# Three raw weight buffers, one buffer of converted words, and the bounds of w of eight units checked later, in an RWKV kernel with two feed-forward layers

## The chip, the cores and the metric

The kernel runs on 1 core of one Trainium2 chip. The metric is the device time of one execution in microseconds. A core has TensorE (PE; its weight loads are listed as PEld), VectorE (DVE), ScalarE (ACT), GpSimd (POOL) and SyncE (SP), which here issues all the DMAs. Each engine works through its own queue in order; an instruction that waits holds up everything behind it on that engine.

## The reference

Inputs are r, k, v, w of shape 4 x 8 x 768 x 48 (batch, heads, sequence, head size), u of 8 x 48, and the weights of two feed-forward layers. The attention keeps a 48 x 48 state for each batch and head:

```python
for t in range(S):
    cur = u * k[t] outer v[t]
    y[t] = r[t] @ (state + cur)
    state = w[t][:, None] * state + k[t] outer v[t]
```

The result, as 3072 tokens by 384, goes through two layers:

```python
h = x @ w_in                     # 384 -> 2048
x = (h - np.tanh(h)) @ w_out     # 2048 -> 384
h = x @ w_in2                    # 384 -> 1024
e = exp(h - max(h)); sm = e / (sum(e) + 1e-9)
solu = h * sm
out = (layernorm(solu) * g_ln) @ w_out2
```

The weights reach the kernel as 64-bit floats.

## The kernel before, in words

**Units and blocks.** The attention is cut into 24 units of 128 tokens and 8 heads (`UB` = 4 units make a block of 512 tokens, `NB` = 6 blocks). A unit u goes through `att_pre` (ruk on GpSimd, its sum dg on VectorE), `att_0` (transposes, the running product inc, its logarithm and exponential kh), `att_1`, `att_2` (the products qk and the transposed keys kt, copied by ScalarE to kn at L319), `att_3` (the state update ds at L328, L329, then L339, L340 on VectorE) and `att_4` (the output y at L354, copied to xs by ScalarE at L359 and VectorE at L360). Units 0 to 3 run in the prologue, from the sorted list `first`. The rest run between the steps of the first layer.

**Steps.** The loop over s has one step for each block i and each of the `NM` = 16 chunks m of 128 hidden columns. `part1` (L395) makes hp with nine matmuls of 128 x 512 (L401): each factor is held as a high and a low part, three products for each of three row groups. Then the nonlinearity is made as a polynomial: t on ScalarE (L406), y on VectorE (L407), a second square on ScalarE (L410), y on VectorE (L412), and a check of the range on ScalarE (L413), whose result is only its accumulated flag. g is split into high and low parts (L415 or L417, and L418 on GpSimd). In the first and the last block L410 writes over hp, in the others a tile with the tag q. `part2` (L421) adds chunk m to x2p two steps later, with nine matmuls (L425). Step s = 0 of unit work and step 0 of the layer are offset so that a unit runs in every four steps.

**Weights.** The 64-bit weights are loaded as words into a raw tile of 128 x 1536 words (`load_pair`, L149; four DMAs of 96 KB at L367 and one of 384 KB at L384) and converted (`convert`, L112). ScalarE rescales the low words in place (L121). VectorE masks and shifts the high words into a PSUM bank (L129, L130) and adds both into a tile of converted words, cv_x (L131), in two halves. ScalarE copies cv_x to the high part of wa (L134) and GpSimd subtracts that from cv_x for the low part (L135). There are two raw tiles (pool `cvr`) and two cv_x tiles (pool `cv`). Conversion m is that of chunk m. Conversions 0 and 1 are in the prologue, conversion s + 2 in step s of the first block (L657, L658), so that `part1` of block 0 follows the conversions closely. From step 16 on the raw tiles take the weights once more for a check of their range (`check_pair`, L143), 24 of them. In the last block the second layer's eight pairs are loaded and converted (`conv_b`, L459) through the same pools; there cv_x serves for the intermediate words too.

**Checks of w.** Bounds of w are checked unit by unit (`check_w`, L239) with two Relu on ScalarE, one for each bound, each with an accumulated flag. For units 0 to 7 (`TURN` = 8) they stand in `att_pre`, on the loaded w, with a scratch tile (cw, ruk or inv) as output; in units 4 to 7 that scratch tile is the one into which GpSimd then writes ruk (L254). From unit 8 on they read the turned w in PSUM (L282). At the end of the first layer the flags are added up, and if one is set, a general path runs in place of the result.

**What sets the order.** The program is traced in the order of the lists and loops; a scheduler then orders each engine's queue by when it estimates that operands and buffers are ready, and adds the waits. `issue_after` puts instructions behind a named one on the same engine. A tile of a pool is reused when all readers of its last content are done. All DMAs are in SyncE's queue, in order.

The last part, from about 560 us, is the second layer for 24 tiles of 128 tokens; its tiles lie where the pools of the first layer were.

Of the kernel before, what the change touches and what calls it, by code (L numbers as in the profile page):

```python
# [33 lines left out]
TURN = 2 * UB  # L34


W_LO, W_HI = 0.75, 1.34
# [21 lines left out]
class Kern:  # L59
# [7 lines left out]
    def setup(self, const):  # L67
        nc = self.nc
        self.ident = const.tile([128, 128], F32, name="ident")
        self.zeros = const.tile([128, 1], F32, name="zeros")  # L70
        self.ub = const.tile([128, H, D], F32, name="ub")
        self.mask = const.tile([128, 4, 128], U8, name="mask")
        self.cst = const.tile([128, 8], F32, name="cst")
        self.nflag = 2 * NU + NB * NM + NM + NM2
        self.flags = const.tile([128, self.nflag], F32, name="flags")
        make_identity(nc, self.ident)
        nc.vector.memset(self.zeros, 0.0)
        for i, val in enumerate((F_SB, -F_T2, W_LO, -W_HI, -0.5, P_SB, P_MIN, FLAG_MIN2)):
            nc.vector.memset(self.cst[:, i:i + 1], val)
        (self.c_fsb, self.c_t2, self.c_lo, self.c_hi, self.c_mhalf, self.c_sb, self.c_min,  # L80
         self.c_flag) = (self.cst[:, i:i + 1] for i in range(8))

    def setup_mask(self, ones):
        nc = self.nc
        nc.gpsimd.memset(ones, 1.0)
        nc.gpsimd.affine_select(
            out=ones, in_=ones, compare_op=ALU.is_gt, fill=0.0, base=0,
            pattern=[[0, 4], [1, 128]], channel_multiplier=-1,
        )
        nc.vector.tensor_copy(self.mask, ones)  # L90
# [21 lines left out]
    def convert(self, pool, raw, hi, lo, scale=None, bank=None):  # L112
# [10 lines left out]
        for i in range(n):  # L123
# [7 lines left out]
            v.tensor_tensor(x[:, s], a, L_[:, s], ALU.add)  # L131
# [11 lines left out]
    def check_pair(self, rpool, n):  # L143

        raw = self.load_pair(rpool, n)
        with self.tc.issue_after(self.last_act.ins):
            self.check(raw, 2 * NU + NB * NM + n)
# [13 lines left out]
    def att_setup(self, att, xp0, xp1):  # L161
# [27 lines left out]
        for t in self.vt:  # L189
            nc.gpsimd.memset(t[:, :, D:64], 0.0)  # L190

# [47 lines left out]
    def check_w(self, u, w, tmp):  # L239
        for i, (b, s) in enumerate(((self.c_lo, -1.0), (self.c_hi, 1.0))):  # L240
            self.nc.scalar.activation(tmp, w, AF.Relu, bias=b, scale=s,
                                      accum_out=self.flags[:, 2 * u + i:2 * u + i + 1])

    def att_pre(self, u):
# [6 lines left out]
        if u < TURN:  # L251
            w = self.gp.tile([128, BLK], F32, tag="q", name="cw")[:, 0:DM].rearrange("p (h d) -> p h d", h=H) if u < UB else ruk
            self.check_w(u, t[:, 2, :, 0:D], w)
# [47 lines left out]
    def att_2(self, u):  # L301
# [11 lines left out]
        for e in range(2):  # L313
            v.copy_predicated(self.aq[:, e], self.mask, ps[e])
# [27 lines left out]
    def att_4(self, u):  # L342
# [16 lines left out]
        nc.scalar.copy(xs[:, 0, :, cols], p[:, 0:KM])  # L359
        v.tensor_tensor(xs[:, 1, :, cols], p[:, 0:KM], xs[:, 0, :, cols], ALU.subtract)  # L360
# [34 lines left out]
    def part1(self, i, m):  # L395
# [7 lines left out]
        q = self.gp.tile([128, BLK], F32, tag="q", name="q")  # L403
# [7 lines left out]
        col = 2 * NU + i * NM + m  # L411
# [9 lines left out]
    def part2(self, i, m, gs):  # L421
# [5 lines left out]
        if m == NM - 1:  # L427
            for d in range(KM):
                o = self.gp.tile([128, BLK], F32, tag="qty"[d], name="x2o")
                self.nc.scalar.activation(o, self.x2p[d], AF.Copy, scale=-1.0)  # L430
                self.nc.sync.dma_start(out=self.x2d[d * 128:(d + 1) * 128, i * BLK:(i + 1) * BLK], in_=o)
# [161 lines left out]
def fast_path(tc, K, const):  # L593
# [9 lines left out]
    cv = pool(L, "cv", 2)  # L603
    cvr = pool(L, "cvr", 2)
# [34 lines left out]
    for s in range(-2, NB * NM + 2):  # L639
# [17 lines left out]
        if 0 <= s < NM - early:  # L657
            K.conv_a(cv, cvr, s + early)  # L658
# [19 lines left out]
        if 0 <= n < NM + NM2 and due < 3:  # L678
# [220 lines left out]
```

## Time and profile before

| | us |
|---|---|
| median of 3 runs | 770.36 (769.48 to 771.55) |
| the profiled execution | 775.22 |
| its span, first to last instruction | 773.4 |
| PE busy | 725.0 (94%) |
| DVE busy | 585.2 (76%) |
| ACT busy | 490.8 (63%) |
| POOL busy | 419.0 (54%) |

Times in the trace count from the start of the span. Busy shares are means over stages that differ: the prologue and the first block (to about 160 us), the other blocks (to about 560 us) and the second layer. PEclk is the granted clock of TensorE as a share of its full 2.4 GHz. The end of a matmul in the trace is modelled, so rows of many matmuls overlap a little.

### The profile page before, as it was taken

To read this page: it belongs to the slowest core of one execution; us is meant where nothing else is said; L and a number is where in the kernel's file an instruction comes from. 1 tells how busy PE (TensorE), PEld (TensorE's weight loads), DVE (VectorE), ACT (ScalarE), POOL (GpSimd) and SP (SyncE) were. 2 spreads that over 40 slices of the span, in tenths; PEclk is the share of its full clock that TensorE was granted. 3 is DMA by queue.
4 is the path that set the end of the run, shared out by engine and by line. 5 is a ranking of instruction groups with operands and counts; after the bars stand their busy time and mean duration, and the time that the engine had idled before them with its cause. 6 is when DMAs were issued, how large, how long until landed. Compare 5 with 4: busy or idle time off the path is not lost.

```text
span 773.4 us, 13992 instructions
## 1 busy us (share of the span) xinstructions
PE 725.0 (94%) x4882; PEld 599.2 (77%) x4882; DVE 585.2 (76%) x999; ACT 490.8 (63%) x920; POOL 419.0 (54%) x397
## 2 busy tenths in 40 slices
PE   6558988999999999999999999999989999999986
PEld 4446667778877888887888887878769989989976
DVE  4868888877766687677677774487669999999992
ACT  4436777588676877686768665787745555554552
POOL 7424575666566666556655654467525454454440
PEclk9879999999999999999999999999999999999999
DMA  9962666666756756576555510232045555555631
GB/s 156 189 127 69 157 185 151 147 169 179 175 146 162 196 143 174 133 205 177 138 154 168 155 62 11 82 123 83 10 158 183 168 178 172 175 169 168 188 104 46
DMA packets 171632, 110.80 MB, mean 143 GB/s; under 512 B 93600, under 2 KB 160288, under 8 KB 171552
## 3 DMA queue, kind: packets, MB, share of 16 engines
q1 hardware_dynamic: 171552, 109.82, 52.9%
q8 instruction: 40, 0.66, 0.4%
q14 instruction: 40, 0.33, 0.1%
HBM read 88.81 MB, written 20.97 MB: 142 GB/s over the span
## 4 chain that ended last, share of the span: by engine, by line
PE 49%; DVE 28%; ACT 10%; DMA 5%; SPq 4%; issue 3%; POOL 1%; ACTq 0%; DVEq 0%; POOLq 0%
PE hp L401 19%; PE x2p L425 19%; DVE tw L539 6%; DVE so L514 4%; PE y L354 4%; DVE e L508 4%; DMA raw<-in_moe_w_out_dram 3%; ACT e L515 3%; DVE part L504 3%; PE qk L312 3%; SPq L367 2%; PE o L564 2%; DVE cv_x L131 2%; SPq L201 1%; PE kt L318 1%
## 5 line engine op out<-in xcount | busy, mean ns | idle before, releaser
L425 PE MATMUL x2p<-g,wa 128*128 128x512 f32 x864 | 226.0, 400 | 9.6 <-ACT g L415 7.9
L401 PE MATMUL hp<-xs,wa 128*128 128x512 f32 x864 | 216.0, 395 | 2.5 <-POOL wa L135 1.3
L425 PEld LDWEIGHTS x2p<-g,wa 128*128 128x128 f32 x864 | 158.7, 189 | 49.6 <-ACT g L415 9.9
L401 PEld LDWEIGHTS hp<-xs,wa 128*128 128x128 f32 x864 | 163.4, 190 | 39.7 <-POOL wa L135 2.3
L418 POOL TENSOR_TENSOR g<-y,g 128x512 fp32r<-128x512 f32 x96 | 129.6, 1351 | 48.4 <-ACT g L415 39.0
L407 DVE TENSOR_TENSOR y<-hp,t 128x512 f32<-128x512 f32 x96 | 65.8, 686 | 76.8 <-ACT t L406 60.4
L564 PE MATMUL o<-wb,ts 128*128 128x384 f32 x576 | 105.1, 336 | 2.5 <-POOL ts L543 2.5
L482 PE MATMUL h<-wb,x2s 128*128 128x512 f32 x432 | 104.1, 392 | 3.2 <-POOL x2s L471 1.7
L413 ACT ACTIVATE q<-t,cst 128x512 f32<-128x512 f32 x96 | 69.5, 724 | 55.7 <-DVE y L412 55.1
L564 PEld LDWEIGHTS o<-wb,ts 128*128 128x128 f32 x576 | 100.7, 188 | 4.8 <-POOL ts L543 3.2
L482 PEld LDWEIGHTS h<-wb,x2s 128*128 128x128 f32 x432 | 80.4, 188 | 20.7 <-POOL x2s L471 2.7
L417 POOL TENSOR_SCALAR g<-y 128x512 fp32r<-128x512 f32 x64 | 40.3, 630 | 81.5 <-DVE y L412 77.4
L406 ACT ACTIVATE t<-hp 128x512 f32<-128x512 f32 x96 | 56.5, 588 | 27.2 <-PE hp L401 26.3
L515 ACT ACTIVATE e<-so 128x1024 f32<-128x1024 f32 x24 | 25.5, 1061 | 59.6 <-DVE so L514 59.6
L543 POOL TENSOR_TENSOR ts<-tw,ts 128x512 fp32r<-128x512 f32 x44 | 55.9, 1292 | 4.4 <-ACT ts L542 4.4
L412 DVE SCALAR_TENSOR_TENSOR y<-q,y 128x512 f32<-128x512 f32 x64 | 51.4, 803 | 2.9
L471 POOL TENSOR_TENSOR x2s<-x2s 128x384 fp32r<-128x384 f32 x24 | 24.4, 1017 | 48.1 <-ACT x2s L470 43.7
L297 POOL TENSOR_TENSOR inv<-inc,kh 112x512 f32<-112x512 f32 x24 | 29.1, 1213 | 37.4 <-ACT kh L289 33.7
L410 ACT ACTIVATE q<-t,cst 128x512 f32<-128x512 f32 x64 | 46.3, 723 | 1.3
L539 DVE STREAM_TRANSPOSE tw<-sw 128x1024 f32<-128x1024 f32 x22 | 44.5, 2022 | 0.4 <-issue 0.3
L517 POOL TENSOR_TENSOR st<-st,cst 128x1 f32<-128x1 f32 x23 | 12.6, 549 | 53.0 <-DVE st L498 45.3
L121 ACT ACTIVATE raw<-raw 128x768 uint32<-128x768 uint32 x24 | 21.8, 908 | 27.9 <-DMA raw<-in_moe_w_out_dram 24.3
(138 smaller groups left out, 1182.4 us busy)
## 6 DMA issues: line engine op xcount, KB each, us to landing
raw<-in_moe_w_out_dram SPq DMA_DIRECT2D x48, 384.0 KB, 4.0
raw<-in_moe_w_in_dram SPq DMA_DIRECT2D x128, 96.0 KB, 2.8
dso<-so SPq DMA_DIRECT2D x22, 512.0 KB, 3.0
sw<-dso SPq DMA_DIRECT2D x88, 128.0 KB, 3.0
rkw<-in_k_dram SPq DMA_DIRECT2D x64, 96.0 KB, 2.7
rkw<-in_r_dram SPq DMA_DIRECT2D x64, 96.0 KB, 2.4
rkw<-in_w_dram SPq DMA_DIRECT2D x64, 96.0 KB, 2.4
raw<-in_moe_w_in_dram SPq DMA_DIRECT2D x16, 384.0 KB, 3.2
```

Of the source, the lines that this page charges most:

```text
L401: self.mm(hp, self.wa[:, a, m, j * 128:(j + 1) * 128], xs[:, b, j], start=n == 0, stop=n == len(seq) - 1)
L406: nc.scalar.activation(t, hp, AF.Square)
L407: v.tensor_tensor(y, hp, t, ALU.mult)
L412: self.last_dve = v.scalar_tensor_tensor(y, p, F_E, y, ALU.add, ALU.mult)
L413: self.last_act = nc.scalar.activation(q, t, AF.Relu, bias=self.c_t2, accum_out=self.flags[:, col:col + 1])
L418: g.tensor_tensor(gs[:, 1], y, gs[:, 0], ALU.subtract)
L425: self.mm(self.x2p[d], self.wa[:, a, m, sl], gs[:, b], start=m == 0 and n == 0, stop=m == NM - 1 and n == 2)
L482: self.mm(p[:, f], xs[:, a, j], w, start=q == 0, stop=q == 8)
L515: nc.scalar.activation(e, so, AF.Square, accum_out=va)
L539: self.turned = nc.vector.transpose(x.rearrange("p k (t b) -> p b k t", b=4), sw)
L543: nc.gpsimd.tensor_tensor(ts[:, 1, k], x[:, k], ts[:, 0, k], ALU.subtract)
L564: self.mm(p, ts[:, a, k], self.wb[:, b, k, DM:], start=q == 0, stop=q == 3 * NM2 - 1)
```

## The change

- The pool of raw tiles has three buffers and that of converted words one.
- Where the bank is not given (second layer), L131 writes the sum into the high words of the raw tile, so that cv_x is free after it; L133, L134 and L135 then read every second word of the raw tile.
- The bounds of w become one: the square of w - 1.045 must not be over 0.087025. It is one Square and one Relu with a flag, in place of two Relu.
- Units 0 to 7 are no longer checked in `att_pre`. Two more `check_pair` (after the 24 for weights) load the w of four units each into a raw tile, with four DMAs, and check 128 x 1536 words with one Square and one Relu.
- Conversion 2 (step s = 0) is traced under `behind()`: its ScalarE instructions stand behind L359 of unit 3 and its VectorE instructions behind L360 of unit 3.
- The tag q has one buffer in place of two.
- The mask is one 128 x 128 tile, broadcast over four in `att_2`; the zeros share a tile with the flags, of which there are fewer.

```diff
--- before.py
+++ after.py
@@ -32,9 +32,10 @@
 RKW = 3 * H * 64
 ROW = 4 * 4 * D
 TURN = 2 * UB
-
-
-W_LO, W_HI = 0.75, 1.34
+NW = NU - TURN + TURN // UB
+
+
+W_MID, W_RAD2 = 1.045, 0.087025
 
 P_MIN = 1e-30
 
@@ -67,17 +68,17 @@
     def setup(self, const):
         nc = self.nc
         self.ident = const.tile([128, 128], F32, name="ident")
-        self.zeros = const.tile([128, 1], F32, name="zeros")
         self.ub = const.tile([128, H, D], F32, name="ub")
-        self.mask = const.tile([128, 4, 128], U8, name="mask")
+        self.mask = const.tile([128, 128], U8, name="mask")
         self.cst = const.tile([128, 8], F32, name="cst")
-        self.nflag = 2 * NU + NB * NM + NM + NM2
-        self.flags = const.tile([128, self.nflag], F32, name="flags")
+        self.nflag = NW + NB * NM + NM + NM2
+        flags = const.tile([128, self.nflag + 1], F32, name="flags")
+        self.flags, self.zeros = flags[:, 0:self.nflag], flags[:, self.nflag:]
         make_identity(nc, self.ident)
         nc.vector.memset(self.zeros, 0.0)
-        for i, val in enumerate((F_SB, -F_T2, W_LO, -W_HI, -0.5, P_SB, P_MIN, FLAG_MIN2)):
+        for i, val in enumerate((F_SB, -F_T2, -W_MID, -W_RAD2, -0.5, P_SB, P_MIN, FLAG_MIN2)):
             nc.vector.memset(self.cst[:, i:i + 1], val)
-        (self.c_fsb, self.c_t2, self.c_lo, self.c_hi, self.c_mhalf, self.c_sb, self.c_min,
+        (self.c_fsb, self.c_t2, self.c_mid, self.c_rad, self.c_mhalf, self.c_sb, self.c_min,
          self.c_flag) = (self.cst[:, i:i + 1] for i in range(8))
 
     def setup_mask(self, ones):
@@ -87,7 +88,7 @@
             out=ones, in_=ones, compare_op=ALU.is_gt, fill=0.0, base=0,
             pattern=[[0, 4], [1, 128]], channel_multiplier=-1,
         )
-        nc.vector.tensor_copy(self.mask, ones)
+        nc.vector.tensor_copy(self.mask, ones[:, 0])
 
     def to_f32(self, pool, raw, out, scale=None, add=None):
 
@@ -128,7 +129,9 @@
                 a = bank.tile([128, 4, C], F32, tag="a", name="cv_a").rearrange("p j t -> p (j t)")[:, 0:DM].bitcast(U32)
             v.tensor_scalar(a, H_[:, s], 3, 0x3FFFFFF8, ALU.logical_shift_left, ALU.bitwise_and)
             v.scalar_tensor_tensor(a, H_[:, s], 0xC0000000, a, ALU.bitwise_and, ALU.bitwise_or)
-            v.tensor_tensor(x[:, s], a, L_[:, s], ALU.add)
+            v.tensor_tensor(H_ if bank is None else x[:, s], a, L_[:, s], ALU.add)
+        if bank is None:
+            xf = H_.bitcast(F32)
         if scale is not None:
             nc.scalar.activation(xf[:, DM:], xf[:, DM:], AF.Copy, scale=scale)
         nc.scalar.copy(hi, xf)
@@ -142,9 +145,20 @@
 
     def check_pair(self, rpool, n):
 
-        raw = self.load_pair(rpool, n)
+        if n < NM + NM2:
+            raw = self.load_pair(rpool, n)
+            with self.tc.issue_after(self.last_act.ins):
+                self.check(raw, NW + NB * NM + n)
+            return
+        h = n - NM - NM2
+        raw = rpool.tile([128, 2, DM, 2], U32, tag="raw", name="raw").rearrange("p i f two -> p (i f two)").bitcast(F32)
+        w = raw.rearrange("p (i h d) -> p i h d", i=UB, h=H)
+        for i in range(UB):
+            b, c = divmod(UB * h + i, NC)
+            self.nc.sync.dma_start(out=w[:, i], in_=self.w[b, :, c * C:(c + 1) * C, :].rearrange("h p d -> p h d"))
         with self.tc.issue_after(self.last_act.ins):
-            self.check(raw, 2 * NU + NB * NM + n)
+            self.nc.scalar.activation(raw, raw, AF.Square, bias=self.c_mid)
+            self.nc.scalar.activation(raw, raw, AF.Relu, bias=self.c_rad, accum_out=self.flags[:, h:h + 1])
 
     def load_pair(self, rpool, n):
 
@@ -189,6 +203,12 @@
         for t in self.vt:
             nc.gpsimd.memset(t[:, :, D:64], 0.0)
 
+    def behind(self):
+        st = ExitStack()
+        for i in self.last3:
+            st.enter_context(self.tc.issue_after(i.ins))
+        return st
+
     def rk(self, u):
         return self.rkw[u if u < UB else u % 2]
 
@@ -237,9 +257,8 @@
         return p
 
     def check_w(self, u, w, tmp):
-        for i, (b, s) in enumerate(((self.c_lo, -1.0), (self.c_hi, 1.0))):
-            self.nc.scalar.activation(tmp, w, AF.Relu, bias=b, scale=s,
-                                      accum_out=self.flags[:, 2 * u + i:2 * u + i + 1])
+        self.nc.scalar.activation(tmp, w, AF.Square, bias=self.c_mid)
+        self.nc.scalar.activation(tmp, tmp, AF.Relu, bias=self.c_rad, accum_out=self.flags[:, u + NW - NU:u + NW - NU + 1])
 
     def att_pre(self, u):
         nc = self.nc
@@ -248,9 +267,6 @@
         ruk = self.ruk
         if u <= UB:
             ruk = self.gp.tile([128, BLK], F32, tag="y", name="ruk")[:, 0:DM].rearrange("p (h d) -> p h d", h=H)
-        if u < TURN:
-            w = self.gp.tile([128, BLK], F32, tag="q", name="cw")[:, 0:DM].rearrange("p (h d) -> p h d", h=H) if u < UB else ruk
-            self.check_w(u, t[:, 2, :, 0:D], w)
         nc.gpsimd.tensor_tensor(ruk, r, self.ub, ALU.mult)
         nc.gpsimd.tensor_tensor(ruk, k, ruk, ALU.mult)
         nc.vector.reduce_sum(self.dg[u % 2].rearrange("p e j -> p j e"), ruk.rearrange("p (j e) d -> p j e d", e=2), axis=AX)
@@ -311,7 +327,7 @@
                 s = slice(64 * e, 64 * e + D)
                 self.mm(ps[e][:, j], kh[s, j], rh[s, j], start=True, stop=True)
         for e in range(2):
-            v.copy_predicated(self.aq[:, e], self.mask, ps[e])
+            v.copy_predicated(self.aq[:, e], self.mask.unsqueeze(1).to_broadcast([128, 4, C]), ps[e])
         if u % NC < NC - 1:
             p = self.bank(u, "kt")[:, :, 0:NP]
             for j in range(4):
@@ -356,8 +372,10 @@
         if u == UB:
             self.xs.append(self.xp1.tile([128, 2, KM, BLK], F32R, tag="xs1", name="xs1"))
         xs = self.xs[blk % 2]
-        nc.scalar.copy(xs[:, 0, :, cols], p[:, 0:KM])
-        v.tensor_tensor(xs[:, 1, :, cols], p[:, 0:KM], xs[:, 0, :, cols], ALU.subtract)
+        xhi = nc.scalar.copy(xs[:, 0, :, cols], p[:, 0:KM])
+        xlo = v.tensor_tensor(xs[:, 1, :, cols], p[:, 0:KM], xs[:, 0, :, cols], ALU.subtract)
+        if u == UB - 1:
+            self.last3 = xhi, xlo
 
     def load_w1(self, raw, m):
 
@@ -400,7 +418,7 @@
         for n, (a, b, j) in enumerate(seq):
             self.mm(hp, self.wa[:, a, m, j * 128:(j + 1) * 128], xs[:, b, j], start=n == 0, stop=n == len(seq) - 1)
         t = self.gp.tile([128, BLK], F32, tag="t", name="t")
-        q = self.gp.tile([128, BLK], F32, tag="q", name="q")
+        q = self.gp.tile([128, BLK], F32, tag="q", name="q", bufs=1)
         y = self.gp.tile([128, BLK], F32, tag="y", name="y")
         gs = self.gs.tile([128, 2, BLK], F32R, tag="g", name="g")
         nc.scalar.activation(t, hp, AF.Square)
@@ -408,7 +426,7 @@
         ends = i in (0, NB - 1)
         p = hp if ends else q
         nc.scalar.activation(p, t, AF.Square, bias=self.c_fsb, scale=F_S)
-        col = 2 * NU + i * NM + m
+        col = NW + i * NM + m
         self.last_dve = v.scalar_tensor_tensor(y, p, F_E, y, ALU.add, ALU.mult)
         self.last_act = nc.scalar.activation(q, t, AF.Relu, bias=self.c_t2, accum_out=self.flags[:, col:col + 1])
         if ends:
@@ -426,7 +444,7 @@
                         stop=m == NM - 1 and n == 2)
         if m == NM - 1:
             for d in range(KM):
-                o = self.gp.tile([128, BLK], F32, tag="qty"[d], name="x2o")
+                o = self.gp.tile([128, BLK], F32, tag="qty"[d], name="x2o", bufs=1 if d == 0 else 2)
                 self.nc.scalar.activation(o, self.x2p[d], AF.Copy, scale=-1.0)
                 self.nc.sync.dma_start(out=self.x2d[d * 128:(d + 1) * 128, i * BLK:(i + 1) * BLK], in_=o)
 
@@ -600,8 +618,8 @@
     K.setup(const)
     K.gl = const.tile([128, NM2], F32, name="gl")
     L, R, R2 = ExitStack(), ExitStack(), ExitStack()
-    cv = pool(L, "cv", 2)
-    cvr = pool(L, "cvr", 2)
+    cv = pool(L, "cv", 1)
+    cvr = pool(L, "cvr", 3)
     K.gp = pool(L, "gp", 2)
     K.gs = pool(L, "gs", 3)
     wp = pool(L, "wp")
@@ -655,7 +673,8 @@
         if 0 <= s - 2 < NB * NM:
             K.part2(*divmod(s - 2, NM), gs.pop(s - 2))
         if 0 <= s < NM - early:
-            K.conv_a(cv, cvr, s + early)
+            with K.behind() if s == 0 else nullcontext():
+                K.conv_a(cv, cvr, s + early)
         if s == LAST:
             R.close()
             wb = pool(R2, "wb", side="right")
@@ -675,7 +694,7 @@
             small = K.ub.rearrange("p h d -> p (h d)")
             hs = {0: K.b_h(K.load_x2(0), 0, None, (small[:, 0:8], small[:, 8:40], *big))}
         n, due = divmod(3 * (s - NM), 7)
-        if 0 <= n < NM + NM2 and due < 3:
+        if 0 <= n < NM + NM2 + TURN // UB and due < 3:
             K.check_pair(cvr, n)
     safe = K.safe_flag(const)
     L.close()
```

## Rows read from the trace of the kernel before

**Rows 1.** Windows: stretch in us, length, busy us of the engines, PEclk, DMA share.

```profile
core 0: us, PE busy (x) PEld busy (x) DVE busy (x) ACT busy (x) POOL busy (x), PEclk, DMA share, GB/s
0.00:60.00 60.00, 36.19 (x425) 28.40 (x426) 38.51 (x90) 25.52 (x50) 29.88 (x47) 0.85 0.90 152
60.00:160.00 100.00, 88.50 (x611) 67.42 (x610) 88.49 (x169) 68.82 (x127) 59.09 (x44) 0.95 0.57 146
160.00:480.00 320.00, 319.64 (x2486) 257.90 (x2487) 223.46 (x390) 229.98 (x460) 193.49 (x188) 1.00 0.57 151
480.00:560.00 80.00, 78.91 (x344) 63.93 (x343) 50.83 (x64) 62.77 (x116) 45.63 (x30) 1.00 0.21 72
```

**Rows 2.** The chain that ended last, 0 to 180 us: start, us, what.

```profile
37.19 5.21 DMA raw<-in_moe_w_out_dram
42.51 0.88 ACT raw L121
43.38 0.43 ACT kn L319
...
55.30 0.37 DVE st L339
...
56.89 0.36 DVE st L340
...
80.68 0.89 ACT raw L121
81.57 0.52 ACT g L415
```

**Rows 3.** Waits, 20 to 165 us: us in total, times, longest.

```profile
ACT raw L121 <- DMA raw<-in_moe_w_out_dram: 24.3, 11, 3.9
...
SPq L367 <- DVE cv_x L131: 45.3, 12, 10.1
...
PE ds L328 <- ACT kn L319: 10.2, 2, 7.0
PE x2p L425 <- ACT g L415: 7.9, 6, 2.0
...
POOL ruk L254 <- ACT ruk L241: 8.2, 1, 8.2
```

**Rows 4.** ScalarE's queue in order of time, prologue: start, us, instruction, idle before.

```profile
39.27 0.83 ACT L134 CAST wa<-cv_x 128x768 fp32r<-128x768 f32 x1 [3.56 <-DVE cv_x L131]
...
46.65 0.91 ACT L121 ACTIVATE raw<-raw 128x768 uint32<-128x768 uint32 x1 [2.85 <-DMA raw<-in_moe_w_out_dram]
```

**Rows 5.** TensorE in order of time, first block.

```profile
82.13 4.19 PE L425 MATMUL x2p<-g,wa 128*128 128x512 f32 x9 [1.78 <-ACT g L415]
...
109.23 1.05 PE L425 MATMUL x2p<-g,wa 128*128 128x512 f32 x3 [1.70 <-ACT g L415]
110.08 3.77 PE L401 MATMUL hp<-xs,wa 128*128 128x512 f32 x9
...
134.34 0.97 PE L425 MATMUL x2p<-g,wa 128*128 128x512 f32 x3 [1.90 <-ACT g L415]
136.16 2.34 PE L401 MATMUL hp<-xs,wa 128*128 128x512 f32 x9 [0.85 <-POOL wa L135]
```

**Rows 6.** VectorE and GpSimd in order of time: first and last of four.

```profile
83.27 0.54 DVE L131 CUSTOM_DVE_ANT_0 cv_x<-raw,cv_a 128x768 uint16<-128x768 uint16 x1
83.39 1.84 POOL L135 TENSOR_TENSOR wa<-cv_x,wa 128x768 fp32r<-128x768 f32 x1
...
126.51 0.56 DVE L131 CUSTOM_DVE_ANT_0 cv_x<-raw,cv_a 128x768 uint16<-128x768 uint16 x1 [0.17 <-DVE cv_a L130]
126.74 1.84 POOL L135 TENSOR_TENSOR wa<-cv_x,wa 128x768 fp32r<-128x768 f32 x1
```

**Rows 7.** Groups by form: busy us, mean ns of one, idle before.

```profile
L141 ACT ACTIVATE raw<-raw,cst 128x768 f32<-128x768 f32 x24 | 23.9, 994 | 0.3
...
L135 POOL TENSOR_TENSOR wb<-cv_x,wb 128x768 fp32r<-128x768 f32 x8 | 17.0, 2119 | 3.0 <-PE x2p L425 3.0
...
L241 ACT ACTIVATE cw<-rkw,cst 128x384 f32<-128x384 f32 x8 | 4.9, 616 | 4.7 <-DMA rkw<-in_w_dram 4.6
```

## The prediction

> **What bounds the kernel now.** I read the stretches first, then the chain that ended last, the waits, and the queues of ScalarE, TensorE, VectorE and GpSimd around the waits that matter. The stretches [rows 1] show that TensorE is full from 160 us (319.6 of 320) and nearly so to 560 us; a change that adds no matmul can gain only before 160 us or after 560 us, and after 560 us the diff moves only the places of buffers, for which I take 0. In the first 60 us TensorE is busy for 36.2 us and in the next 100 for 88.5, while VectorE is busy for 88.5 of those 100. The chain [rows 2] names what is late: at 37 us it runs through the transfer of conversion 2's weights, their rescaling L121 on ScalarE and only then the copy kn L319 of unit 2; at 80.7 us again from L121 to g L415. ScalarE's queue is in order, so what stands behind a waiting L121 waits with it. The waits [rows 3] give the sizes between 20 and 165 us: ScalarE stood 24.3 us before L121, SyncE's queue 45.3 us before the weight loads L367, for a raw buffer that VectorE's L131 had not yet freed, and TensorE 7.0 us for unit 2's kn.
>
> **Third raw buffer, prologue.** Conversion 2's load no longer waits for conversion 0's buffer, and its ScalarE and VectorE instructions stand behind unit 3's xs. So L121 at 42.5 us is no longer ahead of kn of unit 2. What is late next is L134 of conversion 1, issued at 39.27 and done by 40.1 [rows 4]: kn could start there and not at 43.4, a gain of 3.3 us. Against it, the five loads of conversion 2 now go out earlier, probably behind those of conversion 1 and in front of six loads of units 4 and 5; the DMA engines are 0.90 busy in the first 60 us [rows 1], so what follows comes later. Unit 4's ruk on GpSimd feeds dg on VectorE, which stands before the second half of conversion 1. Its cover is the wait of 8.2 us in which GpSimd stood before unit 4's ruk for the check L241 [rows 3], and that check is gone. I take -1.5 us, between -3.3 and the rival's price below.
>
> **Third raw buffer, conversions 3 to 15.** Before, the load of conversion m+2 could start only when conversion m had been added up. Now it starts one conversion earlier, so ScalarE should find the words landed. TensorE's waits that go back to a late L121, or to checks in ScalarE's queue behind one, are 1.78 us before 82.13, 1.70 before 109.23, 1.90 before 134.34 and 0.85 before 136.16 [rows 5]: 6.2 us. Right after the first two, nine matmuls took 4.19 and 3.77 us, where nine at 136.16 took 2.34: 3.3 us more. The granted clock of 60 to 160 us is 0.95 [rows 1], so part of it ran at the lower level of 1.2 GHz; without the idle time in front I expect these to go. Together -9.5 us; the other end is 0, if VectorE sets the pace.
>
> **One buffer of converted words.** L131 of a conversion writes the words that L135 of the one before still reads, on GpSimd. In the trace four conversions after 60 us began L131 before that L135 was over. The first is at 83.27, with L135 running from 83.39 for 1.84 us; the last at 126.51, with L135 from 126.74 [rows 6]. Made to wait, these four cost 2.0, 2.5, 2.3 and 2.1 us, 8.8 us of VectorE, whose queue behind L131 holds the y instructions of the main chain. Some of it is filled by other work put in front. Ends 0 and +8.8; I take half, +4.4, as VectorE has 11.5 us idle in these 100.
>
> **The checks of w.** Eight units lose two ScalarE instructions each of 0.62 us [rows 7] and their accumulator reads before 160 us; this is inside the terms above. Two checks of 1536 columns, of two instructions each, come back in the fifth block, before 480 us. From 0.99 us for 768 columns [rows 7] I estimate under 2 us an instruction, some 7 us in all, with 8 loads. ScalarE is busy for 230 of 320 us there and TensorE is full: 0, or +7 if that cover were gone. Later units still have two instructions; the second now needs the first, on the same engine.
>
> **Edits at nothing.** With one q tile, L410 of a step must follow L413 of the step before; ScalarE's order there has room and TensorE holds a backlog. The copies under a broadcast mask: L340 reads a broadcast operand and takes 0.36 us, L339 without one 0.37 [rows 2]. In the second weight set L131 writes, and ScalarE and GpSimd read, every second word. L135 there is 2.12 us, eight times [rows 7], beside 78.9 of 80 us of TensorE and 45.6 of GpSimd [rows 1]. If it doubled it would still fit; the end is +2 us for the last one. The Trainium skill, GPSIMD Engine Reference, "Performance pitfalls for Q7 kernels", adds half to reads with a step over 8 bytes; here the step is 8, so by that page it adds nothing, and no run here shows it yet.
>
> **Sum.** -1.5 - 9.5 + 4.4 = -6.6 us. The profiled execution took 775.2 us (span 773.4), 4.8 above the median of 770.4, so 768.6 on its scale and 763.8 for the median. A measurement of this kernel can tell about 0.3%, 2.3 us, from no change.
>
> **Rival 1: the fourth conversion takes the third's place.** Only conversion 2 is held back. Conversion 3 now gets conversion 0's buffer, as conversion 2 did, so its L121 may be queued where that one stood, ahead of kn. The DMA engines were nearly full up to there, so its words land no sooner than before: L121 of conversion 3 ran at 46.65 [rows 4]. Then kn starts near 47.4 in place of 43.4: +4.0, and with -5.1 from the block -1.1, 769.3 us. For it: the same order of events as before. Against: its place was one behind kn before, at 46.65. The Trainium skill, DMA: Bandwidth & Descriptors, "Issuing engines are not separate DMA queues", says that all transfers share the same 16 engines, so that an earlier load takes its time from later ones; by that rule this rival's landing time holds, and the trace agrees with a share of 0.90. Chance 0.16.
>
> **Rival 2, slower: the one buffer of words becomes the bound.** Place: VectorE's L131 behind GpSimd's L135 in conversions 3 to 15. VectorE's 88.5 us of work plus 8.8 of new waits plus its 11.5 of old ones would make the stretch 108.8 us, +8.8; if the 6.2 us that come from late words go, +2.6. Middle +5.7, 776.1 us. It decides once the wait for L135 exceeds what the earlier loads save on VectorE. Against: L131 twice, L134 and L135 need about 4 us, while a step takes over 6. Chance 0.14.
>
> **Rival 3: nothing is given back.** -3.3 - 9.5 = -12.8, 757.6 us; it needs VectorE's order to hide the four waits. Chance 0.14.
>
> **Rival 4: the transfers were hidden anyway.** VectorE's pace holds and ScalarE only waits elsewhere: 770.4 us. For it: 88% of VectorE. Against: its idle time follows TensorE and ScalarE. Chance 0.06.
>
> **How the numbers follow.** The forecast has 0.50, with 760 to 768 as its own range. Faster by over 0.3% (below 768.1): nearly all of 0.50, rival 3, a quarter of rival 1, 0.66. Slower (above 772.7): rival 2 and the tails of rivals 1 and 4, 0.18. Within: 0.16. The range of 756 to 774 takes in rivals 1, 3 and 4 and the low end of rival 2.
>
> **What would show it.** Right: ds L328 no longer waits 7 us for kn; ScalarE's wait before L121 is under 8 us in 20 to 165; L367's wait in SyncE's queue falls by more than half; TensorE is full from about 153 us; a new wait of VectorE's L131 for L135 stands at 3 to 6 us. Wrong: L121 of conversion 3 ahead of kn of unit 2 (rival 1); L131 waits of 8 us or more (rival 2); gaps of TensorE after 160 us, from the one q tile or the late checks.

## The result, and the profile after

| kernel | median, us | executions | range, us | ratio to before, 95% interval |
|---|---|---|---|---|
| before | 771.55 | 5 | 769.48 to 774.88 | |
| after | 781.56 | 5 | 774.69 to 783.14 | 1.0103 [1.0071, 1.0135] |

The change made the kernel slower by 1.0% in the ratio on record; the medians lie 10 us apart. The forecast was 6.6 us faster. The execution that the profile of after shows is the shortest of its five: 774.69 us, with a mean granted clock of 0.984. The other four took 781.24 to 783.14 at 0.967 to 0.975. So the page of after hides the loss, and a second trace of the same kernel (a_look2 below, 782.62 us at 0.969) is read beside it. The page of before errs the other way: its execution took 775.22 us, more than any of the five here. The two pages are 0.4 us apart in span (773.4 and 773.0); side by side they show how the order of the work changed, not what the change costs.

In the names below L122 is the rescaling of raw words on ScalarE (L121 before), L132 the last word instruction on VectorE (L131), L137 and L138 the rounding on ScalarE and the subtraction on GpSimd (L134, L135), L344 ds (L328), L375 and L376 xs (L359, L360), L335 kn (L319), L419 and L443 the two matmuls of a step (L401, L425), L424 and L433 t and g (L406, L415), L385 the weight load (L367).

The windows of the profile after, with the columns of [rows 1]:

```profile
0.00:60.00 60.00, 35.35 (x408) 27.29 (x408) 37.70 (x89) 17.94 (x27) 29.34 (x47) 0.86 0.97 165
60.00:160.00 100.00, 88.70 (x628) 67.88 (x629) 89.25 (x171) 66.42 (x119) 60.03 (x45) 0.98 0.58 147
160.00:480.00 320.00, 320.00 (x2484) 257.84 (x2483) 222.61 (x389) 231.59 (x447) 189.95 (x187) 1.00 0.59 155
480.00:560.00 80.00, 79.28 (x348) 64.65 (x347) 49.91 (x66) 65.31 (x118) 47.43 (x31) 1.00 0.18 62
```

Beside [rows 1] ScalarE has 7.6 us less work in the first stretch, where the checks stood, and TensorE is no busier: 35.4 us where it was 36.2, and 88.7 where it was 88.5. From 160 us on nothing has changed. The waits of the profile after, 20 to 165 us, answer to [rows 3]:

```profile
ACT raw L122 <- DMA raw<-in_moe_w_out_dram: 28.2, 11, 6.3
...
PE ds L344 <- ACT kn L335: 9.1, 2, 5.7
...
PE x2p L443 <- ACT g L433: 5.8, 4, 2.3
...
ACT raw L122 <- DMA raw<-in_moe_w_in_dram: 4.7, 1, 4.7
...
PE hp L419 <- POOL wa L138: 3.8, 4, 1.6
...
DVE cv_x L132 <- POOL wa L138: 1.0, 2, 0.8
```

ScalarE stands before L122 for 28.2 us for words that have not landed, and for 4.7 more for those of the other half; [rows 3] has 24.3 of the first kind. SyncE's queue waits for L132 nearly as long as ever:

```profile
SPq L385 <- DVE cv_x L132: 41.4, 13, 9.2
```

The reason is in ScalarE's queue of the profile after (start, us, instruction, idle before):

```profile
41.23 0.53 ACT L335 COPY kn<-x2p 128x448 f32<-128x448 f32 x1
46.42 0.92 ACT L122 ACTIVATE raw<-raw 128x768 uint32<-128x768 uint32 x1 [4.66 <-DMA raw<-in_moe_w_in_dram]
50.38 0.88 ACT L122 ACTIVATE raw<-raw 128x768 uint32<-128x768 uint32 x1 [3.05 <-DMA raw<-in_moe_w_out_dram]
51.16 0.46 ACT L375 CAST xs<-y 128x384 fp32r<-128x384 f32 x1
51.52 0.53 ACT L335 COPY kn<-x2p 128x448 f32<-128x448 f32 x1
56.80 0.48 ACT L375 CAST xs<-x2p 128x384 fp32r<-128x384 f32 x1 [0.68 <-PE x2p L370]
57.18 0.92 ACT L122 ACTIVATE raw<-raw 128x768 uint32<-128x768 uint32 x1
```

Unit 2's kn does come earlier, at 41.23 where ScalarE's queue of before has it at 43.29 (43.38 in [rows 2], which counts from the end of the L121 ahead of it). But conversions 3 and 4, which nothing holds back, now stand directly behind it: the L122 at 46.42 and 50.38 belong to them, and that of conversion 2, held back by the change, follows only at 57.18. Both wait for a landing, and xs of unit 2 and kn of unit 3 wait behind them. Their loads in SyncE's queue of the profile after:

```profile
35.62 1.92 SPq L385 DMA_DIRECT2D raw<-in_moe_w_in_dram  x4
...
38.12 2.16 SPq L385 DMA_DIRECT2D raw<-in_moe_w_in_dram  x4
...
43.23 2.01 SPq L385 DMA_DIRECT2D raw<-in_moe_w_in_dram  x4
...
66.39 2.78 SPq L385 DMA_DIRECT2D raw<-in_moe_w_in_dram  x4
```

These are conversions 2 to 5. Conversions 2 to 4 in the profile before:

```profile
35.28 1.87 SPq L367 DMA_DIRECT2D raw<-in_moe_w_in_dram  x4
...
39.91 1.86 SPq L367 DMA_DIRECT2D raw<-in_moe_w_in_dram  x4
...
65.58 3.28 SPq L367 DMA_DIRECT2D raw<-in_moe_w_in_dram  x4
```

Conversion 4's load went out 22 us earlier (43.23, 65.58), and its L122 went earlier with it.

The same holds all through the first block. This is the place of L122 in ScalarE's queue, counted in steps: how many t and g instructions stand ahead of it.

```
conversion   2    3    4    5    6    7    8    9    10   11
before      0/0  0/0  2/1  3/2  4/4  5/4  6/5  7/6  8/7  9/8
after       0/0  0/0  0/0  2/1  3/2  4/4  5/4  6/5  7/6  8/8
held        1/0  2/0  3/2  4/3  5/4  6/5  7/6  8/7  9/8  10/9
```

From conversion 3 on, each conversion of after stands where before has the conversion ahead of it (to within one g): the lead that the third buffer gives to a load is taken back by the queue. (The row "held" is an experiment below.)

### The profile page after: what moved, and what is told of

Read it like the earlier page. It is cut to its first block, busy times and chain, and to the rows that moved or that the text cites. A ratio compares the mean times of both kernels' runs of the same rounds, so it can differ in the third digit from the quotient of the medians.

```text
span 773.0 us, 13962 instructions
## 1 busy us (share of the span) xinstructions
PE 725.1 (94%) x4882; PEld 599.0 (77%) x4882; DVE 583.3 (75%) x999; ACT 484.6 (63%) x878; POOL 417.8 (54%) x397
## 4 chain that ended last, share of the span: by engine, by line
PE 49%; DVE 28%; ACT 8%; DMA 6%; SPq 4%; issue 3%; POOL 1%; ACTq 0%; DVEq 0%
PE x2p L443 19%; PE hp L419 19%; DVE tw L557 6%; DVE so L532 4%; DVE e L526 4%; PE y L370 4%; DMA raw<-in_moe_w_out_dram 3%; ACT e L533 3%; DVE part L522 3%; PE qk L328 3%; DMA raw<-in_moe_w_in_dram 2%; PE o L582 2%; SPq L221 1%; SPq L385 1%; DVE raw L132 1%
## 5 line engine op out<-in xcount | busy, mean ns | idle before, releaser
L443 PE MATMUL x2p<-g,wa 128*128 128x512 f32 x864 | 223.4, 399 | 7.3 <-ACT g L433 5.8
L419 PE MATMUL hp<-xs,wa 128*128 128x512 f32 x864 | 213.7, 392 | 4.4 <-POOL wa L138 3.8
L443 PEld LDWEIGHTS x2p<-g,wa 128*128 128x128 f32 x864 | 159.3, 189 | 47.0 <-ACT g L433 7.2
L419 PEld LDWEIGHTS hp<-xs,wa 128*128 128x128 f32 x864 | 160.9, 188 | 41.0 <-POOL wa L138 5.3
L436 POOL TENSOR_TENSOR g<-y,g 128x512 fp32r<-128x512 f32 x96 | 127.9, 1332 | 50.0 <-ACT g L433 40.2
L425 DVE TENSOR_TENSOR y<-hp,t 128x512 f32<-128x512 f32 x96 | 66.0, 688 | 87.5 <-ACT t L424 70.7
L431 ACT ACTIVATE q<-t,cst 128x512 f32<-128x512 f32 x96 | 69.4, 723 | 59.0 <-DVE y L430 58.3
L424 ACT ACTIVATE t<-hp 128x512 f32<-128x512 f32 x96 | 56.5, 590 | 20.3 <-PE hp L419 19.3
L122 ACT ACTIVATE raw<-raw 128x768 uint32<-128x768 uint32 x24 | 21.8, 907 | 34.8 <-DMA raw<-in_moe_w_out_dram 28.4
L138 POOL TENSOR_TENSOR wa<-cv_x,wa 128x768 fp32r<-128x768 f32 x16 | 29.3, 1832 | 21.2 <-ACT wa L137 21.2
```

The lines of the kernel that those rows point to most:

```text
L419: self.mm(hp, self.wa[:, a, m, j * 128:(j + 1) * 128], xs[:, b, j], start=n == 0, stop=n == len(seq) - 1)
L424: nc.scalar.activation(t, hp, AF.Square)
L425: v.tensor_tensor(y, hp, t, ALU.mult)
L431: self.last_act = nc.scalar.activation(q, t, AF.Relu, bias=self.c_t2, accum_out=self.flags[:, col:col + 1])
L436: g.tensor_tensor(gs[:, 1], y, gs[:, 0], ALU.subtract)
L443: self.mm(self.x2p[d], self.wa[:, a, m, sl], gs[:, b], start=m == 0 and n == 0, stop=m == NM - 1 and n == 2)
```

## The experiments

Two causes stood against each other at first: L122, too early in ScalarE's queue, spends the lead of the third raw buffer, so that holding it back returns the gain; or the one buffer of converted words costs the time, and the third raw buffer has nothing to give.

### The change again, and single parts of it

a_again is the changed kernel as it is.

> The changed kernel once more, to see where its longer executions (about 781 us, granted clock 0.97, against 774.7 and 0.984 in the profile at hand) lose their time. Theory A (fourth and fifth conversions' rescaling ahead of unit 2's xs and unit 3's kn in ScalarE's queue, so that TensorE idles in the prologue): a long execution shows its extra 7 us before 60 us, with a granted clock there under 0.86. Theory B (one buffer of converted words sets the pace): the extra time lies between 60 and 165 us, with waits of VectorE's add for GpSimd's subtraction of 8 us or more. Theory C (one q tile, late checks): TensorE has gaps after 165 us. Under every theory the median is 779 to 783.

Measured: 777.72 us (774.75 to 782.44, 6 executions) beside 773.33 of the kernel before, 1.0074 [1.0049, 1.0099]; the 779 to 783 us expected under every theory was a little too high. Its mean granted clock goes with its time again: 774.75 us at 0.986, 782.44 at 0.969.

a_hold3 holds conversions 3 and 4 back as the change holds conversion 2:

```diff
-            with K.behind() if s == 0 else nullcontext():
+            with K.behind() if s < 3 else nullcontext():
```

> The changed kernel with the conversions 3 and 4 held behind unit 3 as well, on both engines. Theory A: the waits of 4.7 and 3.1 us before their rescaling no longer stand ahead of unit 2's xs and unit 3's kn; the first matmul of the first layer starts near 52 us and not 57, and the median falls by 4 to 8 us, to 773 to 777. Theory B: no more than 1 us, 780 to 782, as the block's pace takes the gain back. Theory C: the same as B.

Measured: 774.73 us, 1.0019 [0.9999, 1.0038], 3.0 us below a_again, and the two intervals do not meet: 773 to 777 was what theory A gave. The first layer's first t starts at 60.1 us (63.5 in the profile after), but its seventeenth at 162.2 (162.4 there): in this pair of traces, both of executions near 774 us, what the prologue gave was lost again in the first block, where L122 still stands one conversion early.

a_raw2 takes the third raw buffer away:

```diff
-    cvr = pool(L, "cvr", 3)
+    cvr = pool(L, "cvr", 2)
```

> The changed kernel with two raw buffers, all else as changed. Theory A: only one of the two early rescalings is left ahead of unit 2's xs, so 2 to 5 us faster than the changed kernel, 776 to 780. Theory B: the loads again wait for the buffers and the one buffer of words stays, so slower than the changed kernel by 1 to 5 us, 782 to 787. Theory C: no change against the changed kernel, 780 to 783.

Measured: 780.17 us, 1.0091 [1.0063, 1.0120]. The interval overlaps that of the change: without the third raw buffer the kernel is no different by what can be told. Its L122 stand again where before has them (conversion 4 at 2/1, conversion 5 at 3/2, in the count above): the place moves with the raw buffers.

b_words1 is the kernel before with one buffer of words:

```diff
-    cv = pool(L, "cv", 2)
+    cv = pool(L, "cv", 1)
```

> The kernel before with one buffer of converted words in place of two, nothing else. Theory B: slower than before by 5 us or more, 776 or over, with VectorE's add waiting for GpSimd's subtraction in the first block. Theory A and theory C: within 2 us of before, 769 to 773.

Measured: 783.59 us, 1.0114 [1.0073, 1.0155]. The trace splits it. At the seventeenth t it is 2.2 us behind before (164.9, 162.7), though at the ninth it had been 8.8 behind (122.7, 113.9). From the last t of the trace to the end it takes 223.2 us where before takes 215.2. The last rounding of the second weight set comes 16 us later there (564.4, 548.4). This kernel has the words of that set in the one buffer while the change has them in the raw tile, and after takes 215.1 us from its last t to the end, so this part of the loss is not the change's.

### Both buffers back, and L122 held

a_look1 and a_look2 are the changed kernel, for two more traces.

> The changed kernel, one look, to have the trace of one of its usual executions (777 to 783 us, granted clock 0.967 to 0.977); the two traces at hand are both of 774.7 us. Theory B' (the pace of the first block hangs on conversions that wait for each other, and a short idle time of TensorE there costs a stretch at its lower clock): a long execution has the same order and the same waits, with TensorE at the lower level for some 10 us more between 60 and 165 us. Theory A: the extra time is before 60 us. Theory C: after 165 us.

> The same, a second look. Theory B': extra time between 60 and 165 us at the lower clock. Theory A: before 60 us. Theory C: after 165 us.

Measured: 777.34 and 782.62 us, granted clock 0.975 and 0.969. The starts of t in the first block say where the time is lost:

| trace | first t | ninth t | 17th t | span |
|---|---|---|---|---|
| before | 63.3 | 113.9 | 162.7 | 773.4 |
| after | 63.5 | 116.5 | 162.4 | 773.0 |
| a_look1 | 65.3 | 118.8 | 166.8 | 775.5 |
| a_look2 | 67.4 | 120.9 | 170.0 | 780.9 |
| a_raw2 | 62.2 | 112.9 | 162.6 | 777.2 |
| a_bufs_back | 62.1 | 110.4 | 158.6 | 770.8 |
| a_hold_all | 59.9 | 107.7 | 157.8 | 770.0 |
| a_hold_raw2 | 61.1 | 109.0 | 157.4 | 767.9 |

From the 17th t to the end a_look2 takes 610.9 us and before 610.7. All of the 7.5 us by which its span exceeds that of before are lost earlier, 4.1 of them ahead of the first t. ScalarE's queue of a_look2 there:

```profile
40.70 0.53 ACT L335 COPY kn<-x2p 128x448 f32<-128x448 f32 x1
48.01 0.93 ACT L122 ACTIVATE raw<-raw 128x768 uint32<-128x768 uint32 x1 [6.78 <-DMA raw<-in_moe_w_in_dram]
52.11 0.88 ACT L122 ACTIVATE raw<-raw 128x768 uint32<-128x768 uint32 x1 [3.17 <-DMA raw<-in_moe_w_out_dram]
52.89 0.46 ACT L375 CAST xs<-y 128x384 fp32r<-128x384 f32 x1
```

and TensorE of a_look2 behind it:

```profile
54.00 1.12 PE L287 MATMUL tp<-ident,rkw 128*128 128x128 f32 x4 [4.43 <-DVE xs L376]
...
63.85 5.35 PE L419 MATMUL hp<-xs,wa 128*128 128x512 f32 x16
```

The same two lines of after:

```profile
52.27 1.12 PE L287 MATMUL tp<-ident,rkw 128*128 128x128 f32 x4 [2.94 <-DVE xs L376]
...
61.40 3.91 PE L419 MATMUL hp<-xs,wa 128*128 128x512 f32 x16
```

The words of conversion 3 were rescaled 1.6 us later than in after (48.01, 46.42), xs followed, TensorE stood idle for 4.43 us in place of 2.94, and the next sixteen matmuls of the first layer took 5.35 us in place of 3.91. The windows of TensorE's clock of a_look2 (columns of [rows 1]):

```profile
45.00:50.00 5.00, 4.57 (x68) 3.41 (x60) 0.46 (x1) 0.93 (x1) 1.09 (x1) 0.85 1.12 227
50.00:55.00 5.00, 1.00 (x4) 0.72 (x4) 1.62 (x3) 1.68 (x3) 0.00 (x0) 0.83 0.60 113
55.00:60.00 5.00, 4.41 (x66) 3.25 (x65) 4.14 (x11) 1.89 (x4) 1.27 (x2) 0.50 0.32 62
60.00:65.00 5.00, 5.00 (x25) 3.94 (x26) 2.83 (x5) 1.29 (x2) 2.96 (x3) 0.50 0.11 21
```

and of after:

```profile
45.00:50.00 5.00, 4.33 (x76) 3.40 (x68) 0.88 (x2) 0.92 (x1) 1.09 (x1) 0.96 0.90 198
50.00:55.00 5.00, 2.73 (x29) 1.96 (x29) 3.24 (x8) 1.94 (x4) 0.00 (x0) 0.72 0.51 97
55.00:60.00 5.00, 2.53 (x49) 1.75 (x46) 4.22 (x8) 2.38 (x4) 2.35 (x3) 0.94 0.34 66
60.00:65.00 5.00, 5.00 (x36) 4.18 (x36) 4.09 (x9) 1.95 (x4) 1.88 (x2) 1.00 0.00 0
```

In a_look2 TensorE was busy for 1.00 us of 50 to 55, and from 55 to 65 it ran at 0.50, the lower level of 1.2 GHz, while it was nearly full. In after it was busy for 2.73 us and back at 2.4 GHz by 60. The stall is the change's; it was longer where the words landed later, and what followed it ran at the lower clock. That the stall alone lowered the clock is not shown: from 45 to 50 the two already differed (0.85, 0.96). From 60 to 165 us the clock is 0.90 in a_look2 and 0.98 in after.

a_bufs_back takes both changes of buffers back and leaves the rest:

```diff
-    cv = pool(L, "cv", 1)
-    cvr = pool(L, "cvr", 3)
+    cv = pool(L, "cv", 2)
+    cvr = pool(L, "cvr", 2)
```

> The changed kernel with two raw buffers and two of converted words, as before; the later checks of w, the one q tile, the mask, the hold of conversion 2 and the sum written into the raw tile of the second weight set stay. Theory B: with the second buffer of words back it loses the slowdown, 768 to 774. Theory A: one early rescaling is left ahead of unit 2's xs, so 776 to 780. Theory C: as slow as the changed kernel, 778 to 783.

Measured: 772.25 us, 0.9981 [0.9952, 1.0010]. So the later checks, the one q tile, the one mask and the words in the raw tile cost nothing that can be told, and the loss is that of the buffers. Beside a_raw2, which has one buffer of words and is otherwise the same, it is 7.9 us shorter in the medians, which were taken on two chips (beside 773.33 and 773.69 us of the kernel before). Three raw buffers with two of words were not run. Waits of a_raw2, 20 to 165 us:

```profile
ACT raw L122 <- DMA raw<-in_moe_w_out_dram: 32.9, 13, 6.5
...
PE hp L419 <- POOL wa L138: 4.5, 4, 2.8
```

and of a_bufs_back:

```profile
ACT raw L122 <- DMA raw<-in_moe_w_out_dram: 21.4, 13, 5.9
...
ACT raw L122 <- DMA raw<-in_moe_w_in_dram: 6.0, 1, 6.0
ACT raw L122 <- DMA rkw<-in_w_dram: 2.6, 1, 2.6
...
PE hp L419 <- POOL wa L138: 0.6, 2, 0.4
```

ScalarE stands before L122 about as long in both (32.9 and 30.0 us). TensorE's wait for converted words differs, 4.5 us against 0.6, by about as much as the two traces at the 17th t (162.6 and 158.6). But the two do not match in time: 2.5 of these 4.0 us are there at the ninth t, before which TensorE had waited 0.4 us for words in a_raw2 and 0.2 in a_bufs_back. The longest wait of a_raw2 comes only ahead of the 17th t:

```profile
156.74 5.83 PE L419 MATMUL hp<-xs,wa 128*128 128x512 f32 x18 [2.82 <-POOL wa L138]
```

The buffer itself stops little: L132 waits 1.0 us for L138 in after, and such a wait does not show in a_raw2. In ScalarE's queue of a_raw2 the rounding L137 of the last two conversions has moved back by a step against a_bufs_back, counted as above, but this does not go with one buffer of words as such: in after, which has one, it has not:

```
conversion            14     15
a_bufs_back, L137   13/12  14/13
a_raw2, L137        14/13  15/14
after, L137         13/13  14/13
```

a_hold_all is the changed kernel with L122 of every conversion held, in ScalarE's queue, behind the range check L431 of the step at which the conversion is issued:

```diff
-        nc.scalar.activation(L_, L_, AF.Copy, scale=2.0**-29)
+        with self.tc.issue_after(self.last_act.ins) if hasattr(self, 'last_act') else nullcontext():
+            nc.scalar.activation(L_, L_, AF.Copy, scale=2.0**-29)
```

> The changed kernel with the rescaling of conversion s+2 in each step s of the first block held behind the last range check traced by then on ScalarE, that of step s, so that no rescaling stands in ScalarE's queue ahead of the work of an earlier step. Theory A, extended to the whole block (the third buffer's lead is spent by queueing the rescaling as early as the load allows): ScalarE's waits before the rescaling fall from over 30 us to under 12 in 20 to 165 us, and the time to 768 to 774. Theory B: the waits fall as well but the pace stays with the one buffer of words, 776 to 781.

Measured: 771.49 us, 0.9971 [0.9949, 0.9994]. One ordering edit takes back all that the change lost: L122 now stands one to three steps later than in after, mostly two (the row "held" above). The line added moves all later lines up by one. ScalarE's waits for landings, 20 to 165 us, fall to 7.1 us (theory A gave under 12):

```profile
ACT raw L123 <- DMA raw<-in_moe_w_out_dram: 7.1, 2, 4.6
```

Both theories can be right here: the second buffer of words alone (a_bufs_back) and the held L122 alone (this kernel) each bring the time back.

### Held, with and without the buffers

By then the queue's part was plain, but it was open whether the third raw buffer gives anything once L122 is held. Three kernels on one chip: the held kernel again, the same with two raw buffers, and the same with two raw buffers and two of words (the edits of a_raw2 and a_bufs_back on top of the hold).

> The changed kernel with L122 of every conversion held on ScalarE behind the range check of the step at which it is issued, a second time, as the yardstick of the two runs beside it (three raw buffers, one buffer of words). Queue theory and order theory both: 769 to 773 us, 0.995 to 0.999 of the kernel before; ScalarE's wait before L123 for a landing under 10 us in 20 to 165 us, the first layer's step 16 at 157 to 159 us.

> The same held queue, with two raw buffers in place of three (one buffer of words). Queue theory (the third raw buffer does give a conversion a lead, and the changed kernel only spent it because L122 stood early in ScalarE's queue): without the buffer the landings are late again, ScalarE's wait before L123 is 15 us or more in 20 to 165 us, step 16 comes 3 to 6 us later, 774 to 778 us. Rival, order theory (the hold alone gains, since nothing else in ScalarE's queue then stands behind a landing; the third buffer is worth nothing): within 1.5 us of the kernel beside it, 770 to 773 us.

> The same held queue, with two raw buffers and two buffers of words, as the kernel before has them. Queue theory: two buffers of words give the 4 us or so up to step 16 that they gave without the hold, and two raw buffers take 3 to 6 us: 769 to 775 us, near the kernel with three and one. Order theory: the hold's gain adds to that of the second buffer of words: 764 to 768 us, faster than all others.

Measured, beside 773.39 us of the kernel before:

| kernel | raw buffers | word buffers | median, us | range, us | ratio, 95% interval |
|---|---|---|---|---|---|
| a_hold_all2 | 3 | 1 | 770.81 | 767.87 to 774.08 | 0.9972 [0.9954, 0.9991] |
| a_hold_raw2 | 2 | 1 | 769.53 | 766.55 to 772.01 | 0.9951 [0.9932, 0.9970] |
| a_hold_bufs | 2 | 2 | 772.09 | 766.00 to 777.09 | 0.9996 [0.9969, 1.0023] |

My queue theory falls in its second half. The kernel with two raw buffers and one of words has the shortest median, at least as short as with three; the rival, that the hold alone gains and the third buffer is worth nothing, is what the runs show. Its other half, that the gain of a second buffer of words adds to that of the hold (764 to 768 us), missed: a_hold_bufs took 772.09. The waits of a_hold_raw2, 20 to 165 us:

```profile
PE ds L345 <- ACT kn L336: 6.8, 2, 3.8
PE x2p L444 <- ACT g L434: 5.5, 4, 2.8
ACT raw L123 <- DMA raw<-in_moe_w_in_dram: 5.4, 1, 5.4
...
ACT raw L123 <- DMA raw<-in_moe_w_out_dram: 1.8, 1, 1.8
```

With two raw buffers the words are in time: ScalarE's wait for landings is 7.2 us, where [rows 3] has 24.3 with the same two buffers. The 7.2 us are those of conversions 0 and 1 in the prologue, which the hold leaves alone; no later L123 waits for a landing. ScalarE's queue of this kernel in the prologue:

```profile
40.41 0.53 ACT L336 COPY kn<-x2p 128x448 f32<-128x448 f32 x1
46.33 0.48 ACT L376 CAST xs<-y 128x384 fp32r<-128x384 f32 x1 [5.40 <-PE y L371]
...
62.46 0.90 ACT L123 ACTIVATE raw<-raw 128x768 uint32<-128x768 uint32 x1
```

xs starts at 46.33, as soon as TensorE has its input, where after had it at 51.16, and the L123 at 62.46 waits for nothing.

The last run is the kernel before with that hold and nothing else.

> The kernel before with one edit: the rescaling L121 of every conversion held on ScalarE behind the range check of the step at which it is issued. It has two raw buffers, two of words, early checks and two q tiles, so it differs from the changed kernel with the same hold and both buffers back only by the small edits. If the small edits cost nothing, as predicted: within 0.4% of that kernel's 0.9996, so 0.996 to 1.003, 770 to 775 us. Rival (the small edits, later checks above all, are what let the held kernels pass the kernel before): 776 us or more, over 1.003.

Measured: 770.66 us beside 772.88, 0.9964 [0.9943, 0.9986]. The hold alone brings the kernel before to where it brings the changed one (0.9951 to 0.9972 with one buffer of words): 0.4% there, while the changed kernel, which had lost 0.7 to 1.0%, gains more. Beside a_hold_bufs (0.9996, overlapping) the small edits are again free by what can be told. a_hold_raw2, at 0.9951 of the kernel before, beats both kernels.

## Why the prediction was wrong

**The failed step** is that of the third raw buffer in conversions 3 to 15, "so ScalarE should find the words landed", -9.5 us. It took the wait before L121 for a late transfer. The load did go out one conversion earlier, but L122 was queued one conversion earlier too, and the wait was no shorter (28.2 + 4.7 us, against the sign that I had named, under 8). Its size measures as 780.17 to 777.72 us, -2.5 with overlapping intervals, without the hold, and +1.3, overlapping too, with it: nothing that can be told. The gaps in [rows 5] were real, and g did stand behind a waiting L121; what took the wait away was the place of L121 in the queue, not an earlier load. Even then the term was too large: with no landing waited for after conversion 1, b_hold_all is 2.2 us and a_hold_raw2 3.9 us shorter than the kernel before, not 9.5. That an instruction's place is no fixed thing, and moves when a buffer is added, was nowhere in my sum.

**The prologue**, -1.5 us. Unit 2's kn came 2.1 us earlier, of the 3.3 reckoned, right behind the rounding of conversion 1 as the prediction had it, and TensorE's wait for it fell by half (the first line is of before, the second of after):

```profile
43.85 0.34 PE L328 MATMUL ds<-vt,kn 128*64 128x48 f32 x1 [6.95 <-ACT kn L319]
41.81 0.34 PE L344 MATMUL ds<-vt,kn 128*64 128x48 f32 x1 [3.44 <-ACT kn L335]
```

(The 5.7 us in the waits of after are unit 1's, at 30.34.) So this sign of being right came true. But what was late behind it was unit 2's xs, with the L122 of conversions 3 and 4 ahead of it. That is rival 1's mechanism one instruction on, with two conversions in the place that it gave to one. In place of -1.5 us the traces show the first t at +0.2 (after), +2.0 (a_look1) and +4.1 us (a_look2); rival 1's price was +4.0. I had also put conversion 2's load ahead of units 4 and 5, which was wrong: it stayed where it was, 35.62 and 35.28 us. a_hold3 shows that conversions 3 and 4 are the cause: holding them brings the first t to 60.1.

**One buffer of words**, +4.4 us. Without the hold it costs 7.9 us (a_raw2 against a_bufs_back), within the end of 8.8. With the hold it costs nothing that can be told (769.53 against 772.09). The mechanism was not the one priced: L132 waits 1.0 us for L138, not 3 to 6. Which mechanism it is instead is not shown. The order of ScalarE's queue is a candidate: in a_raw2 the last two roundings stand a step later than in a_bufs_back, and TensorE waits 3.9 us more for words. Against it: after, with one buffer, has them no later, and b_hold_all, with two, has that of conversion 15 at 15/14 without a loss. So rival 2, whose 776.1 us is by chance near the 777.72 of a_again, has the right side and the wrong mechanism.

**The terms at nothing** held. The late checks and the one q tile leave TensorE at 320.0 of 320 us from 160 to 480, and a_bufs_back bounds all small edits together at 0.9952 to 1.0010. The strided words cost GpSimd 34 ns an instruction, 2153 where [rows 7] has 2119 (the groups by form of the profile after):

```profile
L138 POOL TENSOR_TENSOR wb<-raw,wb 128x768 fp32r<-128x768 f32 x8 | 17.2, 2153 | 1.0 <-ACT wb L137 1.0
```

The Trainium skill, GPSIMD Engine Reference, "Performance pitfalls for Q7 kernels", adds half only to reads with a step over 8 bytes; this row, with a step of 8 bytes and 1.6% more, agrees.

**The range**, 756 to 774 us, missed because the large term and its doubt hung on one reading. The end 0 for -9.5 was there, and 0 with the two other dear ends (+4.0 and +8.8) would have been slower by 1.7%; I gave such a sum no chance of its own.

What stays open: how one buffer of words costs its time without the hold. The traces of a_raw2 and a_bufs_back differ by 6.4 us: 4.0 at the 17th t, 3.2 at the last (560.6, 557.4), and another 3.2 from there to the end, which was not followed up. The scheduler orders the other queues anew as well when one edit moves L122, so what the hold gives is shown for the edit, not for that one place alone. In the last block, where the raw tiles hold the second set's words, the third raw buffer does leave a mark: from 480 to 560 us TensorE is busy for 78.35 us in a_hold_all and 76.83 in a_hold_raw2; the medians do not show it. And a_hold_bufs spreads over 766.0 to 777.1 us, more than the other held kernels. Its one trace, a short execution (span 764.2, clock 0.987), has the 17th t at 153.6 us, so two buffers of words may well help there; what its long executions lose was not traced.

## What to carry to other kernels

A wait for a DMA in front of an instruction says that the two are in the wrong order for that moment; it does not say which of them to move. Before adding a buffer so that the load comes earlier, look at what stands behind the waiting instruction on its in-order engine and whether the waiting one is needed yet: here it could stand two steps later at no cost, and with that done neither the third raw buffer nor a second buffer of words made the kernel shorter by what can be told. A prediction of a change to buffers has to ask where each consumer will then stand in its queue, above all the ones that the change does not hold in place.

## What the hardware showed beside that

Two executions of one program, each with a stall of TensorE at the same place, went on differently. With 2.94 us idle ahead of 52 us the granted clock was 0.72 from 50 to 55 us, 0.94 from 55 to 60 and 1.00 (2.4 GHz) from 60 on; with 4.43 us idle ahead of 54 us it was 0.83, then 0.50 (1.2 GHz) from 55 to 65, and sixteen matmuls took 5.35 us against 3.91. The five executions of after took 774.7 to 783.1 us with the mean clock falling from 0.984 to 0.967, and the one profile, of the shortest, showed hardly any of the loss. The kernel before spreads nearly as far when it is run often enough: 769.5 to 777.9 us in the 29 executions beside a_hold_raw2.
